# Thirteen instead of eleven attention jobs transpose by DMA, small passes are merged, and a planner's costs and due times are reset

## The chip, the cores and the metric

One NeuronCore of a Trainium2 chip runs the kernel. The time is the device time of one execution in microseconds; the median of several runs counts. The engines are TensorE (PE, with its weight loads PEld), VectorE (DVE), ScalarE (ACT), GpSimd (POOL), SyncE (SP, which issues the DMAs) and 16 DMA engines.

## The reference

Attention with a decay over 4 batches, 8 heads, 576 rows and 64 columns, then two dense layers over the 2304 rows of 512 columns, with 2048 hidden columns each. All is float32.

```python
log_f = np.log(np.clip(f, 0.0001, 1.0))
cum = np.cumsum(log_f, axis=-1)
scores = q @ k.T / sqrt(D) + cum[:, None] - cum[None, :]   # per batch and head
scores = np.where(causal, -1e9, scores)
scores = scores - np.max(scores, axis=-1, keepdims=True)
attn = np.exp(scores); attn = attn / (attn.sum(-1, keepdims=True) + 1e-9)
x = attn @ v                         # heads side by side: (2304, 512)
h = x @ w1_in;  x = (h / (1 + np.exp(-h))) @ w1_out
h = x @ w2_in;  out = (h * np.cos(h)) @ w2_out
```

## The kernel before

**Work.** A job is two heads of one batch; there are 16 pairs. Each pair has two jobs: "a" for rows 0 to 255 and "b" for the last rows, 256 to 575. A job makes scores, decays, a row maximum, an exponential and a sum, a division, a transpose of the weights and the values product. The dense layers go by blocks j of 256 rows (nine of them) and by pairs p of 128 hidden columns (eight), a step (l, j, p) being 24 products into h and those of the second matrix. Numbers that need more than 16 bits are split into two float16 parts and multiplied in three passes (`PASS`); blocks 0 and 1 of the first layer (`J16`) multiply by the second matrix in float32 instead.

**Two kinds of "b" jobs.** `BY_DMA` says which. A job by DMA splits the divided weights into float16 parts (`f_hi`, `f_lo`), transposes them with `dma_start_transpose` on SP's queue (lines 841 and 844, six per job), splits the values, and multiplies in float16 (line 937). The others transpose on TensorE in float32 (lines 810 and 813, 19 products), copy the result out of PSUM, and multiply in float32 (line 948). Before, jobs 0 to 5, 6, 8, 10, 12 and 14 go by DMA.

**Order.** All work is handed to a `Scheduler` as tasks with an engine (or several, `alts`), an assumed duration, dependencies, tokens for buffers (`TOK`) and a key; the smallest key that is ready goes first on each engine. It simulates the run while the kernel is built and so writes out a fixed order for each engine; the hardware only waits on semaphores. The steps of the dense layers have keys from -1000 up and so go before the elementwise work of attention. On TensorE the attention products go first. Where the simulation finds TensorE without work in the first 60 us, it writes a filler product there (`keep_warm`, line 410). `apt` and `better` choose the engine for a task that several can run; `EXTRA` is an extra price of an engine, and before `EARLY` us VectorE takes no such task from another engine. `DSLOW` and `PSLOW` are its assumption for VectorE and GpSimd running beside each other.

**Weights.** They come as 64-bit words, are turned into float32 by a few integer passes (`convert`: lines 479 to 492), squared and summed for a scale, and split. First-layer weights have the key CK0 + CK1 * i for the i-th tile (four tiles per pair p). The second layer's are converted in the background, written to DRAM and loaded again; their i-th load waits for the step W2N0 + int(W2N1 * i) of the first layer.

**Scales.** `scale_tasks` adds two sums of squares, sums them over the partitions with a one-column product (line 429), and makes a power of two and its inverse out of it with three passes on VectorE (lines 434 to 436). `balance` does the like for q and k of a "b" job (lines 593 to 600).

**Decays.** f is clipped, its logarithm taken, and a prefix sum scanned over all 576 columns (lines 447 to 460); the first four "a" jobs read it through a product with a selector (line 768), all others from DRAM.

Of the kernel before, what the change touches and what calls it, by code (L numbers as in the profile page):

```python
# [9 lines left out]
F32 = mybir.dt.float32  # L10
F16 = mybir.dt.float16
BF16 = mybir.dt.bfloat16
# [9 lines left out]
NP = B * H // 2  # L22
# [7 lines left out]
BY_DMA = [n < 6 or n % 2 == 0 for n in range(NP)]  # L30
# [25 lines left out]
KO = {"gs": 1.5, "g2": 1.5, "gl2": 1.5, "cb2": 0.5, "cb3": 0.5, "chi": -2.5, "g": -5.5}  # L56
HAM = 3.4133
# [3 lines left out]
EXTRA = {"DVE": 1.2, "POOL": 0.8}  # L61
# [6 lines left out]
EARLY, LATE = 20, ()  # L68
KDEC, KDP = 12.0, -0.5
# [10 lines left out]
class Scheduler:  # L80
# [35 lines left out]
    def run(self):  # L116
# [56 lines left out]
        while events:  # L173
# [23 lines left out]
            while progress:  # L197
                progress = False
                for e in ENG:
# [41 lines left out]
                    if e == "PE":  # L241
                        w = int(now / HAM)
                        while win < w:
                            warm = work[win] > 0.7 * HAM
                            win += 1
                            if len(work) <= win:
                                work.append(0.0)
                        if not warm:
                            end += best.dur
                        a = now  # L250
                        while a < end - 1e-9:
                            w = int(a / HAM + 1e-9)
# [58 lines left out]
def c_dma(mb):  # L311
    return 0.01 + mb / 0.41
# [3 lines left out]
def decay_attention_silu_cos_kernel(ctx, tc, qa, qb, f, w1i, w1o, w2i, w2o, out):  # L316
# [81 lines left out]
    qe = sb.tile([128, 4], I32, name="qe")  # L398
# [20 lines left out]
    def scale_tasks(i, deps, key, top=15, turns=None):  # L419


        cell = {}

        def f_add():
            nc.vector.scalar_tensor_tensor(sq16[:, i:i + 1], sq[:, 0, i:i + 1], 2.0 ** -60, sq[:, 1, i:i + 1], ALU.max, ALU.add)

        def f_sum():
            cell["n"] = ps.tile([128, 512], F32, tag="s", bufs=TOK["s"], name="nrm")
            nc.tensor.matmul(cell["n"][:, 0:1], ones16, sq16[:, i:i + 1], start=True, stop=True, skip_group_check=True)

        def f_two():
            n = cell["n"][:, 0:1].bitcast(I32)
            a, b = scl[:, i:i + 1].bitcast(I32), inv[:, i:i + 1].bitcast(I32)
            nc.vector.tensor_scalar(b, n, 1, 0x3F800000, ALU.logical_shift_right, ALU.bitwise_and)  # L434
# [12 lines left out]
    def d_ln():  # L447
        nc.vector.tensor_scalar(fc[0:32, 0:S], fc[0:32, 0:S], 1e-4, 1.0, ALU.max, ALU.min)

    def d_scan():  # L450
        nc.vector.tensor_tensor_scan(cum[0:32, 0:S], ones[0:32, 0:S], lf[0:32, 0:S], 0.0, ALU.mult, ALU.add)
        nc.vector.tensor_scalar(cum[0:32, 0:S], cum[0:32, 0:S], -8.0, None, ALU.mult)
# [4 lines left out]
    d1 = add("DVE", 0.95, d_ln, [d0], key=-100)  # L457
    d2 = add("ACT", 0.7, lambda: nc.scalar.activation(lf[0:32, 0:S], fc[0:32, 0:S], AF.Ln), [d1], key=-100)
    add("ACT", 1.4, lambda: nc.scalar.activation(spare, halfpi, AF.Exp), [d2], key=-99)
    d3 = add("DVE", 1.95, d_scan, [d2, dm, dz], key=-100)  # L460
    decay = add("SP", 0.5, lambda: nc.sync.dma_start(decay_d, cum[0:32, 0:S]), [d3], key=KDEC, dma=0.3, name="rows")
    scanned = d3

# [41 lines left out]
    for i in range(2 * NF):  # L505
# [5 lines left out]
        def load(c=c, kind=kind, src=src):  # L511
# [5 lines left out]
                         [decay] if kind == "o" and c >= NF - NT_ else [], kind == "o")  # L517
# [37 lines left out]
    def load_tasks(jb, u):  # L555
# [5 lines left out]
        def tile_of(tag):  # L561
            n, dt = {"qk": (QK, F32), "v": (QB - RB, F32), "dk": (QB, F32)}[tag]
            if beta:
                return sbt(tag, [128, n], dt, name=tag)
            if not half:
                pairs[tag, jb.n // 2] = sbt(tag, [128, n], dt, name=tag)
            return pairs[tag, jb.n // 2]
# [23 lines left out]
        def balance():  # L591
            n, c = jb.n, slice(jb.n, jb.n + 1)
            nc.vector.tensor_scalar(qe[:, 0:nq], jb.qn[:, 0:nq].bitcast(I32), 2, 0x1F800000, ALU.logical_shift_right, ALU.bitwise_and)
            sq_, sk = qsc[:, 0, c].bitcast(I32), qsc[:, 1, c].bitcast(I32)
            nc.vector.scalar_tensor_tensor(sq_, qe[:, 1:2], float(127 << 23), qe[:, 0:1], ALU.add, ALU.subtract)
            nc.vector.tensor_scalar(sk, sq_, -1.0, float(254 << 23), ALU.mult, ALU.add)
# [7 lines left out]
        def norm():  # L604
            jb.qn = ps.tile([128, 512], F32, tag="s", bufs=TOK["s"], name="nrm")
            nc.tensor.matmul(jb.qn[:, 0:nq], ones16, qn.bitcast(BF16).rearrange("p n (c t) -> p n c t", t=2)[:, jb.n, 0:nq, 1], start=True, stop=True, skip_group_check=True)
# [45 lines left out]
        own = beta or not half  # L652
        t0 = add("SP", 0.5, load, key=u, acq=["qs"] if beta else ["qk"] if own else [],
                 deps=[] if own else [jb.mate.loads[2]], dma=c_dma(0.49 if beta else 0.26), name="ldq")
        tv = add("SP", 0.5, load_v, key=u + 0.1, acq=["v"] if own else [], deps=[] if own else [jb.mate.loads[0]],
# [47 lines left out]
        if not beta and jb.n < NS_:  # L703
            if half:
                values.append([tv, jb.mate.loads[0]])
            jb.loads, jb.masked = [tv, tv, t0], {"c01": [masked]}
            return [tl]
        t1 = add("SP", 0.5, decays, [decay] + ([] if own else [jb.mate.loads[1]]), key=u, acq=["dk"] if own else [],
                 dma=1.3 if beta else 1.1, name="ldd")
        jb.loads = [tv, t1, t0]  # L710
# [311 lines left out]
    w1_done, sc1 = {}, []  # L1022
    for p in range(NPR):
        k, key = SW(1, "o", p), C16 + C161 * p
        q = [add(**squares(lambda c=c: wo32[c]["w"], 512, sq[:, c % 2, k:k + 1]), deps=wready[1, "o", c], key=key, name="sqw")
             for c in (2 * p, 2 * p + 1)]
        ts = scale_tasks(k, q, key, 14)
        sc1.append(ts)
# [9 lines left out]
    def f_v1():  # L1038
        i, o = SW(1, "i", 0), SW(1, "o", 0)
        nc.vector.tensor_tensor(v1[:, 0], scl[:, i:i + NPR], scl[:, o:o + NPR], ALU.mult)  # L1040
# [4 lines left out]
    factors1 = add("DVE", 0.9, f_v1, sc1 + [wready[1, "i", 2 * p][0] for p in range(NPR)], key=-500, name="sc")  # L1045
# [4 lines left out]
    for i in range(2 * NF):  # L1050
# [17 lines left out]
        ts = scale_tasks(k, [halves[c - 1][2], halves[c][2]], key, *((15, by) if kind == "i" else (14,)))  # L1068
# [38 lines left out]
    def f_v():  # L1107
        i, o = SW(2, "i", 0), SW(2, "o", 0)
        nc.vector.tensor_tensor(v2[:, 0], scl[:, i:i + NPR], scl[:, o:o + NPR], ALU.mult)
# [4 lines left out]
    factors2 = add("DVE", 0.6, f_v, sc2, key=-500, name="sc")  # L1114
# [47 lines left out]
    def factor_tasks(l, j, ts, key):  # L1162
# [20 lines left out]
        if j < 2:  # L1183
            return [add("DVE", 0.1, f1(p, p + 1), [ts, wts[p]], key=key, name="sc") for p in range(NPR)]
        t = add("DVE", 0.1, f1(0, NPR), [ts] + wts, key=key, name="sc")
# [331 lines left out]
```

## Time and profile before

| | us |
|---|---|
| median of three runs | 912.09 (912.05 to 913.18) |
| the profiled execution | 911.74 |
| its span | 909.9 |

| engine | busy us | share of the span | instructions |
|---|---|---|---|
| TensorE, products | 899.1 | 99% | 7928 |
| TensorE, weight loads | 753.0 | 83% | 7928 |
| VectorE | 760.6 | 84% | 1854 |
| ScalarE | 694.9 | 76% | 1425 |
| GpSimd | 160.7 | 18% | 236 |

A product's end is modelled, so its length says less than the distance of starts. A row of a timeline merges neighbours of one kind: the start of the first, the length until the end of the last, and their count. In brackets stands how long the engine had been idle before, and what ended that. A float32 product counts as two instructions.

### The profile page before, as it was taken

What the parts mean: (1) busy time and instruction counts of PE and PEld (TensorE: products, weight loads), DVE (VectorE), ACT (ScalarE), POOL (GpSimd) and SP (SyncE); (2) the same over time, 40 slices, a digit from 0 to 9 for tenths busy, and PEclk for the clock granted to TensorE, in tenths of its full rate; (3) what the DMA queues carried; (4) which work ended last, traced back from release to release, by engine and by line L of the source; (5) the groups of instructions that cost most, each with busy time, mean ns of one, the idle gap of its engine ahead of it and who ended that gap; (6) DMA issues with size and microseconds to landing.
All of it is one profiled execution on the core that took longest, in us unless ns stands there. A gap on an engine that the chain in (4) does not pass through costs nothing.

```text
span 909.9 us, 20973 instructions
## 1 busy us (share of the span) xinstructions
PE 899.1 (99%) x7928; PEld 753.0 (83%) x7928; DVE 760.6 (84%) x1854; ACT 694.9 (76%) x1425; POOL 160.7 (18%) x236
## 2 busy tenths in 40 slices
PE   9999999999999999999999999999999999999997
PEld 5667777788887888887888888888888888888886
DVE  6899878987876999988899987888888888787775
ACT  7999999876868888788797767766676666666663
POOL 6652321133212324323120100000000000000000
PEclk9999999999999999999999999999999999999999
DMA  8965744967987878886674997000001000000010
GB/s 318 372 223 160 235 151 82 196 142 162 202 191 204 213 215 209 209 191 177 221 233 157 317 355 237 24 24 24 24 24 48 24 24 24 1 25 24 1 24 24
DMA packets 113701, 130.03 MB, mean 143 GB/s; under 512 B 63872, under 2 KB 76160, under 8 KB 113600
## 3 DMA queue, kind: packets, MB, share of 16 engines
q1 hardware_dynamic: 113600, 128.70, 49.2%
q8 instruction: 62, 1.02, 0.5%
q14 instruction: 39, 0.32, 0.1%
HBM read 90.25 MB, written 24.72 MB: 126 GB/s over the span
## 4 chain that ended last, share of the span: by engine, by line
PE 93%; ACT 3%; DVE 2%; DMA 1%; issue 1%; DVEq 0%; ACTq 0%; SPq 0%
PE h L1329 40%; PE y L1441 20%; PE y L1220 18%; PE pv L948 2%; PE spin L410 2%; PE st L762 2%; PE tt L810 2%; PE pv L937 2%; PE st L755 1%; ACT junk L358 1%; PE st L743 1%; PE st L768 1%; DMA rw<-w1i 1%; PE st L742 1%; PE h L1318 0%
## 5 line engine op out<-in xcount | busy, mean ns | idle before, releaser
L1329 PE MATMUL h<-x,wi 128*128 128x256 f16 x3432 | 404.6, 273 | 0.0
L1329 PEld LDWEIGHTS <-wi 128*128 128x128 f16 x3432 | 331.6, 98 | 46.6 <-issue 6.5
L1441 PE MATMUL y<-g,rw 128*128 128x256 f16 (+1 forms) x1600 | 224.1, 292 | 2.7 <-ACT g L333 2.7
L1220 PE MATMUL y<-wo,g 128*128 128x256 f16 x1512 | 176.5, 273 | 0.0
L1220 PEld LDWEIGHTS <-g 128*128 128x128 f16 x1512 | 147.9, 98 | 17.1
L1441 PEld LDWEIGHTS <-rw 128*128 128x128 f16 x1344 | 129.2, 98 | 18.3 <-issue 3.3
L793 ACT ACTIVATE e<-e,su 128x128 f32<-128x128 f32 (+4 forms) x144 | 82.9, 578 | 14.4 <-DVE su L772 14.2
L1383 ACT ACTIVATE t<-h,ru 128x512 f32<-128x512 f32 x72 | 49.2, 684 | 57.8 <-PE h L1329 57.5
L1408 DVE TENSOR_TENSOR g<-t,g 128x896 f16<-128x896 f32 x72 | 78.4, 1089 | 14.9 <-ACT g L1405 13.1
L1405 ACT ACTIVATE g<-t 128x896 f16<-128x896 f32 x72 | 68.0, 944 | 28.8 <-DVE t L1399 28.7
L1393 DVE SCALAR_TENSOR_TENSOR t<-h,rg,t 128x512 f32<-128x512 f32 x72 | 54.0, 749 | 34.7 <-ACT t L1390 34.7
L1389 ACT ACTIVATE t<-t,ru 128x512 f32<-128x512 f32 x72 | 51.7, 717 | 26.7 <-DVE t L1386 26.7
L1354 ACT ACTIVATE t<-h,rg 128x512 f32<-128x512 f32 x72 | 48.9, 680 | 29.3 <-PE h L1329 28.9
L333 ACT ACTIVATE g<-t,rg 128x512 f16<-128x512 f32 (+1 forms) x72 | 51.6, 716 | 22.2 <-PE y L1441 19.4
L772 DVE CUSTOM_DVE_ANT_0 e<-st,dk 128x256 f32<-128x256 f32 (+3 forms) x128 | 59.2, 492 | 8.4 <-PE st L762 3.3
L1386 DVE SCALAR_TENSOR_TENSOR t<-t,ru,h 128x512 f32<-128x512 f32 x72 | 53.5, 743 | 8.9 <-ACT t L1383 8.9
L1357 DVE SCALAR_TENSOR_TENSOR t<-t,h 128x512 f32<-128x512 f32 x72 | 49.2, 683 | 11.9 <-ACT t L1354 11.6
L1441 PEld LDWEIGHTS y<-g,rw 128*128 128x128 f32 x256 | 47.0, 194 | 13.1 <-ACT g L333 3.9
L353 DVE SCALAR_TENSOR_TENSOR g<-t,rg,g 128x512 f16<-128x512 f32 x56 | 43.3, 773 | 13.4 <-ACT g L333 12.8
L1390 ACT ACTIVATE t<-t,halfpi 128x512 f32<-128x512 f32 x72 | 52.0, 722 | 2.3
L834 DVE SCALAR_TENSOR_TENSOR eh<-e,su,eh 128x512 f16<-128x512 f32 (+1 forms) x66 | 41.6, 657 | 1.1 <-ACT eh L333 0.6
L333 ACT ACTIVATE e<-e,su 128x256 f32<-128x256 f32 (+4 forms) x78 | 35.2, 509 | 0.9 <-DVE inv L434 0.5
(158 smaller groups left out, 1260.7 us busy)
## 6 DMA issues: line engine op xcount, KB each, us to landing
rw<-w1i SPq DMA_DIRECT2D x16, 512.0 KB, 5.4
rw<-w1o SPq DMA_DIRECT2D x16, 512.0 KB, 7.3
x<-x_d SPq DMA_DIRECT2D x16, 512.0 KB, 4.2
dk<-decay_d SPq DMA_DIRECT2D x16, 512.0 KB, 4.9
raw<-w2i SPq DMA_DIRECT2D x16, 512.0 KB, 5.0
raw<-w2o SPq DMA_DIRECT2D x16, 512.0 KB, 4.2
qs<-qb SPq DMA_DIRECT2D x16, 480.0 KB, 4.2
w2o_d<-w SPq DMA_DIRECT2D x24, 256.0 KB, 3.3
```

Of the source, the lines that this page charges most:

```text
L333: nc.scalar.activation(dst, src, AF.Copy, scale=scale)
L772: nc.vector.tensor_tensor_reduce(out, s, d, -0.125, first, ALU.add, ALU.min, cell["sm"][:, o:o + 1])
L793: nc.scalar.activation(x, x, AF.Exp, bias=sm[:, i:i + 1], scale=-1.0, accum_out=sm[:, 4 + i:5 + i])
L1220: nc.tensor.matmul(y[bank][:, 256 * half:256 * half + 256], g[:, gi, ga], w[:, wi, 256 * col:256 * col + 256], start=p == 0 and half == 0 ...
L1329: nc.tensor.matmul(h[:, i], w[:, wi, 128 * k:128 * k + 128], x[:, xi, k], start=(i == 0 and q == 0 and k == 0), stop=(i == 1 and q == 2 an ...
L1386: nc.vector.scalar_tensor_tensor(cell["t"], cell["t"], r, cell["h"], ALU.subtract, ALU.subtract)
L1389: nc.scalar.activation(cell["t"], cell["t"], AF.Abs, scale=r)
L1390: nc.scalar.activation(cell["t"], cell["t"], AF.Sin, scale=-2.0 * PI, bias=halfpi)
L1393: nc.vector.scalar_tensor_tensor(cell["t"], cell["h"], r, cell["t"], ALU.mult, ALU.mult)
L1405: nc.scalar.activation(g_t[s][:, 0], cell["w"], AF.Copy)
L1408: nc.vector.tensor_tensor(g_t[s][:, 1], cell["w"], g_t[s][:, 0], ALU.subtract)
L1441: nc.tensor.matmul(y[:, e * TB:(e + 1) * TB], w[:, wi, 128 * ec:128 * ec + 128], g[:, gi, i * TB:(i + 1) * TB], start=(st and e == 0), sto ...
```

## The change

- `BY_DMA`: jobs 7 and 9 go by DMA too, 13 of 16.
- `scale_tasks` can do n scales at once and leave the inverse for later (`late`). The scales of the first layer's second matrix are made four at a time (two products instead of eight), and their inverses and those of the second layer in one call each, in `f_v1` and `f_v`.
- `balance` makes q's and k's scale in one pass: the norm product writes its columns twice.
- Clip, logarithm and prefix sum go in two parts, columns 0 to 255 first; the selector products wait for the first part alone.
- The buffers of "a" jobs are taken by tasks of their own with an early key.
- "b" jobs have a key lower by `LEAD` = 1, and their three units are `USTEP` = 1.5 apart instead of 2. `GAP4`, a pause of keys before the second batch of "a" jobs, goes from 8 to 5.
- The planner's numbers: extra price of GpSimd 0.8 to 2.0, `EARLY` 20 to 60, keys of weights, key offsets by name (`KO`), a window for its clock model shifted by `HAM0`.

```diff
-BY_DMA = [n < 6 or n % 2 == 0 for n in range(NP)]
+BY_DMA = [n < 11 or n % 2 == 0 for n in range(NP)]
-LOOK = 12
+LOOK = 13
-QD = 3
+QD = 4.0
-CK2 = 12
+CK2 = 18
-GAP4, GAP8 = 8, 12
-CK0, CK1 = 10, 1.6
-C2K0, C2K1 = 150, 0.5
-W2N0, W2N1 = 30, 1.0
-J16, C16, C161 = 2, 70, 2.0
+GAP4, GAP8 = 5, 12
+CK0, CK1 = 12, 1.8
+C2K0, C2K1 = 210, 0.2
+W2N0, W2N1 = 37, 0.8
+J16, C16, C161 = 2, 65.0, 3.5
-KO = {"gs": 1.5, "g2": 1.5, "gl2": 1.5, "cb2": 0.5, "cb3": 0.5, "chi": -2.5, "g": -5.5}
-HAM = 3.4133
+KO = {"gs": 1.5, "g2": 1.5, "gl2": 1.5, "cb2": 1.5, "cb3": 1.0, "chi": 1.0, "g": -6.5, "max": -3.0, "ldq": -0.5, "exp": 0.5, "xc": 4, "nm": -3.0, "rec": -4, "clo": -2.0, "ws": 4, "qhi": 4, "sqw": -0.5, "cb1": 4, "ldd": -0.5, "hide": 1.5, "tc": 0.5, "vhi": 4, "cexp": 1.5, "qlo": 0.5}
+HAM, HAM0 = 3.4133, 1.3
-EXTRA = {"DVE": 1.2, "POOL": 0.8}
+EXTRA = {"DVE": 1.2, "POOL": 2.0}
-EARLY, LATE = 20, ()
-KDEC, KDP = 12.0, -0.5
+EARLY, LATE = 60, ()
+KDEC, KDP = 6, 0.5
+LEAD, USTEP, GAPB = 1, 1.5, 0
...
-    def scale_tasks(i, deps, key, top=15, turns=None):
+    def inverse(i, n, top):
+        b = inv[:, i:i + n].bitcast(I32)
+        nc.vector.tensor_scalar(b, b, 1.0, float((65 - top) << 23), ALU.mult, ALU.add)
+
+    def scale_tasks(i, deps, key, top=15, turns=None, n=1, late=False):
...
-            nc.vector.tensor_scalar(b, b, 1.0, float((65 - top) << 23), ALU.mult, ALU.add)
+            if not late:
+                inverse(i, n, top)
...
+    def d_scan(a, b):
+        def f():
+            nc.vector.tensor_tensor_scan(tot[0:32, a:b], ones[0:32, a:b], lf[0:32, a:b],
+                                         tot[0:32, a - 1:a] if a else 0.0, ALU.mult, ALU.add)
+            nc.vector.tensor_scalar(cum[0:32, a:b], tot[0:32, a:b], -8.0, None, ALU.mult)
+        return f
...
+    scanned = add("DVE", 0.9, d_scan(0, 256), [d2, dm, dz], key=-100)
...
-            sp = load_tasks(jb, pos)
+            sp = load_tasks(jb, pos - (LEAD if kind == "b" else 0))
...
-                    un += unit_tasks(jb, u, pos + 2 * i, sp, [])
+                    un += unit_tasks(jb, u, pos + USTEP * i, sp, [])
...
+            ts = scale_tasks(k, q, C16 + C161 * (p + NQ - 1), 14, n=NQ, late=True)
```

## Rows read from the trace of the kernel before

**Rows 1.** Stretches: busy PE, PEld, DVE, ACT, POOL (instructions), clock, DMA share, GB/s.

```profile
7.00:30.00 23.00, 23.00 (x148) 14.27 (x146) 17.13 (x61) 19.82 (x62) 16.44 (x20) 1.00 1.00 368
...
66.50:75.00 8.50, 5.01 (x18) 3.87 (x18) 8.19 (x27) 8.50 (x24) 2.85 (x4) 0.80 0.62 189
...
75.00:130.00 55.00, 55.00 (x417) 43.06 (x415) 45.19 (x156) 54.87 (x165) 15.19 (x22) 1.00 0.58 171
130.00:446.00 316.00, 316.00 (x2866) 255.03 (x2864) 271.09 (x742) 257.23 (x576) 89.70 (x140) 1.00 0.77 186
446.00:555.00 109.00, 108.93 (x1009) 97.20 (x1008) 95.50 (x227) 82.26 (x157) 12.21 (x16) 1.00 0.78 265
555.00:902.60 347.60, 347.26 (x3186) 310.90 (x3184) 283.95 (x544) 231.42 (x334) 0.00 (x0) 1.00 0.09 29
```

**Rows 2.** TensorE's timeline around 188 and 278 to 293: start, length, what.

```profile
188.56 1.97 PE L1441 MATMUL y<-g,rw 128*128 128x256 f32 x8
...
278.50 1.87 PE L937 MATMUL pv<-pt 128*64 128x320 f16 x30
280.30 1.09 PE L810 MATMUL tt<-ident,e 128*128 128x128 f32 x8
281.23 0.27 PE L742 MATMUL st<-qk 128*128 128x256 f16 x1
...
290.47 2.42 PE L948 MATMUL pv<-pt,v 128*64 128x320 f32 x20
292.82 0.82 PE L762 MATMUL st<-qk 64*128 64x512 f16 x6
```

**Rows 3.** Line 410 (fillers) by stretch: PE, PEld, clock, DMA share, GB/s.

```profile
0.00:30.00 30.00, 16.88 (x60) 6.18 (x60) 1.00 0.92 326
30.00:46.00 16.00, 7.42 (x29) 2.68 (x29) 1.00 1.00 385
```

**Rows 4.** TensorE's timeline around the hole at 66 to 75.

```profile
58.12 2.86 PE L1441 MATMUL y<-g,rw 128*128 128x256 f32 x12
60.81 0.82 PE L810 MATMUL tt<-ident,e 128*128 128x128 f32 x6
...
67.33 0.16 PE L429 MATMUL nrm<-sq,ones 128*128 128x1 bf16 x1 [1.01 <-DVE inv L434]
70.15 4.54 PE L1441 MATMUL y<-g,rw 128*128 128x256 f32 x12 [2.65 <-ACT g L333]
```

**Rows 5.** DMA issues of the whole run: count, median us to landing.

```profile
pt<-eh SPq DMA_TRANSPOSE x66, 3.4
```

**Rows 6.** VectorE by line, 225 to 450: count, busy us, mean ns.

```profile
L834 DVE SCALAR_TENSOR_TENSOR eh<-e,su,eh 128x512 f16<-128x512 f32 (+2 forms) x42 | 26.3, 651 | 0.8 <-POOL eh L335 0.5 <-ACT eh L333 0.3
...
L700 DVE SCALAR_TENSOR_TENSOR pt<-v,scl,pt 128x512 f16<-128x512 f32 (+1 forms) x12 | 6.3, 568 | 0.3 <-ACT pt L333 0.3
...
L596 DVE TENSOR_SCALAR qsc<-qsc 128x1 int32<-128x1 int32 x10 | 1.5, 154 | 0.3
```

**Rows 7.** VectorE's timeline at the start.

```profile
2.73 0.94 DVE L448 TENSOR_SCALAR fc<-fc 32x576 f32<-32x576 f32 x1 [1.24 <-DMA fc<-f]
4.49 1.48 DVE L451 TENSOR_TENSOR_SCAN cum<-ones,lf 32x576 f32<-32x576 f32 x1 [0.82 <-ACT lf L458]
6.00 0.45 DVE L452 TENSOR_SCALAR cum<-cum 32x576 f32<-32x576 f32 x1
```

**Rows 8.** TensorE's timeline, 6.8 to 9.

```profile
6.87 2.12 PE L410 MATMUL spin<-ones 128*128 128x512 bf16 x9
8.82 1.47 PE L768 MATMUL st<-cum,sel 128*128 128x128 f32 x8
```

**Rows 9.** Chain that ended last, before 80 us: start, us, what.

```profile
52.51 5.45 DMA rw<-w1i
```

**Rows 10.** Line 335, 60 to 200 us, sum of the stretches.

```profile
sum 140.00, DVE 2.99 POOL 15.47; mean DVE 0.43 POOL 2.21
```

**Rows 11.** Line 1058, loads of the second layer: issue, first and last start.

```profile
L1058 SPq DMA_DIRECT2D raw<-w2i x16: 332/422/802, 275.0 to 510.2; - x16
```

More of the change, by code (lines that the diff above doesn't have):

```diff
@@ L241, in run @@
                     if e == "PE":
-                        w = int(now / HAM)
+                        w = int((now + HAM0) / HAM)
                         while win < w:
@@ L427, in f_sum @@
         def f_sum():
             cell["n"] = ps.tile([128, 512], F32, tag="s", bufs=TOK["s"], name="nrm")
[L429 removed]
+            nc.tensor.matmul(cell["n"][:, 0:n], ones16, sq16[:, i:i + n], start=True, stop=True, skip_group_check=True)
         def f_two():
[L432 to L434 removed]
+            m = cell["n"][:, 0:n].bitcast(I32)
@@ L440, in scale_tasks @@
         t = add("PE", 0.04, f_sum, [t], key=key - 10000.0, acq=["s"], name="sc")
-        return add("DVE", 0.46, f_two, [t], key=key, rel=["s"], name="sc")
+        return add("DVE", 0.31 if late else 0.46, f_two, [t], key=key, rel=["s"], name="sc")
     fc, lf, ones, cum = [sb.tile([128, 1024], F32, tag=f"wo{NF - NT_ + i}", bufs=1, name=n)
                          for i, n in enumerate(("fc", "lf", "ones", "cum"))]
-    def d_ln():
-        nc.vector.tensor_scalar(fc[0:32, 0:S], fc[0:32, 0:S], 1e-4, 1.0, ALU.max, ALU.min)
@@ L516, in decay_attention_silu_cos_kernel @@
                          dict(rel=["raw"]) if kind == "i" else dict(rel=["lo"]), [],
-                         [decay] if kind == "o" and c >= NF - NT_ else [], kind == "o")
+                         [decay] if kind == "o" and (c >= NF - NT_ or c == NF - NT_ - 2) else [], kind == "o")
         if kind == "o" and c >= NF - NT_ - 1:
@@ L564, in tile_of @@
                 return sbt(tag, [128, n], dt, name=tag)
-            if not half:
+            if (tag, jb.n // 2) not in pairs:
                 pairs[tag, jb.n // 2] = sbt(tag, [128, n], dt, name=tag)
@@ L605, in norm @@
             jb.qn = ps.tile([128, 512], F32, tag="s", bufs=TOK["s"], name="nrm")
-            nc.tensor.matmul(jb.qn[:, 0:nq], ones16, qn.bitcast(BF16).rearrange("p n (c t) -> p n c t", t=2)[:, jb.n, 0:nq, 1], start=True, stop=True, skip_group_check=True)
+            n = qn.bitcast(BF16).rearrange("p n (c t) -> p n c t", t=2)[:, jb.n, 0:nq, 1]
+            nc.tensor.matmul(jb.qn[:, 0:2 * nq], ones16, n.unsqueeze(1).to_broadcast([128, 2, nq]), start=True, stop=True,
+                             skip_group_check=True)
         def rows(a, heads, count, copies):
@@ L650, in decayt @@
                 nc.sync.dma_start(jb.dt[64 * a:64 * a + 64], rows(a, 1, S, 64))
[L652 to L655, printed above, removed]
+        at = {}
+        if not beta:
+            at = jb.mate.at if half else {tag: add("SP", 0.0, lambda: None, key=u - 300, acq=[tag], name="at")
+                                          for tag in (["qk", "v", "dk"] if jb.n >= NS_ else ["qk", "v"])}
+            jb.at = at
+        t0 = add("SP", 0.5, load, key=u, acq=["qs"] if beta else [], deps=[] if beta else [at["qk"]],
+                 dma=c_dma(0.49 if beta else 0.26), name="ldq")
+        tv = add("SP", 0.5, load_v, key=u + 0.1, acq=["v"] if beta else [], deps=[] if beta else [at["v"]],
                  dma=c_dma(0.33 if beta else 0.13), name="ldq")
@@ L704, in load_tasks @@
             if half:
-                values.append([tv, jb.mate.loads[0]])
-            jb.loads, jb.masked = [tv, tv, t0], {"c01": [masked]}
+                values.append([tv, jb.mate.tv])
+            jb.tv, jb.masked = tv, {"c01": [masked]}
             return [tl]
-        t1 = add("SP", 0.5, decays, [decay] + ([] if own else [jb.mate.loads[1]]), key=u, acq=["dk"] if own else [],
+        t1 = add("SP", 0.5, decays, [decay] + ([] if beta else [at["dk"]]), key=u, acq=["dk"] if beta else [],
                  dma=1.3 if beta else 1.1, name="ldd")
-        jb.loads = [tv, t1, t0]
         r = [tl, tv, t1]
@@ L997, in decay_attention_silu_cos_kernel @@
             mate = jb
-            sp = load_tasks(jb, pos)
+            if kind == "b" and jb.n == 0:
+                pos += GAPB
+            sp = load_tasks(jb, pos - (LEAD if kind == "b" else 0))
             if kind == "a":
@@ L1022, in decay_attention_silu_cos_kernel @@
     w1_done, sc1 = {}, []
+    NQ = 4
     for p in range(NPR):
         k, key = SW(1, "o", p), C16 + C161 * p
[L1025 to L1028, printed above, removed]
+        if p % NQ == 0:
+            q = [add(**squares(lambda c=c: wo32[c]["w"], 512, sq[:, c % 2, k + c // 2 - p:k + c // 2 - p + 1]),
+                     deps=wready[1, "o", c], key=C16 + C161 * (c // 2), name="sqw") for c in range(2 * p, 2 * p + 2 * NQ)]
+            ts = scale_tasks(k, q, C16 + C161 * (p + NQ - 1), 14, n=NQ, late=True)
+            sc1.append(ts)
         for c in (2 * p, 2 * p + 1):
@@ L1044, in f_v1 @@
         nc.vector.tensor_scalar(rg3, v1[:, 1], vm[:, 2:3], 2.0 ** -16, ALU.mult, ALU.mult)
-    factors1 = add("DVE", 0.9, f_v1, sc1 + [wready[1, "i", 2 * p][0] for p in range(NPR)], key=-500, name="sc")
+    factors1 = add("DVE", 1.05, f_v1, sc1 + [wready[1, "i", 2 * p][0] for p in range(NPR)], key=-500, name="sc")
     w2_done = {}
@@ L1067, in decay_attention_silu_cos_kernel @@
         by = sq2[:, p:p + 1] if kind == "i" else scl[:, k:k + 1]
-        ts = scale_tasks(k, [halves[c - 1][2], halves[c][2]], key, *((15, by) if kind == "i" else (14,)))
+        ts = scale_tasks(k, [halves[c - 1][2], halves[c][2]], key, *((15, by) if kind == "i" else (14,)), late=True)
         sc2.append(ts)
@@ L1113, in f_v @@
         nc.vector.tensor_scalar(rg2, v2[:, 1], vm[:, 0:1], 2.0 ** -16 / INV2PI, ALU.mult, ALU.mult)
-    factors2 = add("DVE", 0.6, f_v, sc2, key=-500, name="sc")
+    factors2 = add("DVE", 1.2, f_v, sc2, key=-500, name="sc")
     steps = {}
@@ L1183, in factor_tasks @@
         if j < 2:
-            return [add("DVE", 0.1, f1(p, p + 1), [ts, wts[p]], key=key, name="sc") for p in range(NPR)]
-        t = add("DVE", 0.1, f1(0, NPR), [ts] + wts, key=key, name="sc")
+            return [add("DVE", 0.2, f1(p, p + 1), [ts, wts[p]], key=key, name="sc") for p in range(NPR)]
+        t = add("DVE", 0.2, f1(0, NPR), [ts] + wts, key=key, name="sc")
         return [t] * NPR
```

41 lines of the change are left out of this document (24 added, 17 removed).

## The prediction

> **What bounds the kernel now.** I read the busy times by stretch first, then TensorE's timeline. In the table by stretch the reader is to see one engine without holes: TensorE is busy 55.00 of 55.00 us from 75 to 130, 316.00 of 316.00 from 130 to 446, 108.93 of 109.00 from 446 to 555 and 347.26 of 347.60 from there to its last product, at a granted clock of 1.00 [rows 1]. So from 75 us on nothing but TensorE's own work sets the end, and an edit counts there only if it takes products away, or if it makes something so late that a hole opens.
>
> The share of busy time alone would not prove that, since ends of products are modelled. By the Trainium skill's Perfetto Trace Analysis, section Identifying the Most-Contended Engine, a busy matmul row is a poor measure of headroom. By that rule removed products might give nothing back; the starts in the timeline decide against it here: 30 products of a values pass begin at 278.50 and the next group begins at 280.30, at once behind them, with no idle time noted [rows 2].
>
> Before 75 us it is otherwise. TensorE is kept busy there with filler products (line 410) that compute nothing: 60 of them up to 30 us and 29 more up to 46 us, 16.88 and 7.42 us of busy time. In the same time the DMA engines are busy 0.92 and 1.00 of the time [rows 3], and ScalarE 19.82 of 23 us from 7 to 30 us [rows 1]: the start is held by loads, by ScalarE and by the chain of the first jobs. From 66.5 to 75 us the clock falls to 0.80 [rows 1]. The timeline shows how: TensorE is idle for 1.01 us before the second of two norm products, then 2.65 us for ScalarE's g, and 12 products of the second matrix last 4.54 us where 12 such, 58.12 to 60.81, had needed 2.69 [rows 4]. That hole costs 1.01 + 2.65 + (4.54 - 2.69) = 5.5 us. The clock stood at its 2.4 GHz level before it, and the 12 products behind it ran in good part at the 1.2 GHz level.
>
> **The change part by part.**
>
> Two more jobs (7 and 9) over the crossbar. Such a job drops its 19 transposes on TensorE, and its float32 values pass becomes the float16 one. In the job shown, 8 transposes go from 280.30 to 281.23, 0.116 us each; 19 are 2.2 us. Its float32 values pass goes from 290.47 to 292.82, 2.35 us; the float16 pass takes 280.30 - 278.50 = 1.80 us [rows 2]. The score products are the same in both kinds. Per job 2.2 + 2.35 - 1.80 = 2.75 us less, for two jobs 5.5 us, all of it on the path by rows 1. I take -5.5; the lower bound is 0, if TensorE must wait in their place.
>
> What these jobs add lies beside TensorE. Six crossbar transfers each, 3.4 us from issue to landing, on SP's queue [rows 5]; behind them on that queue wait loads of later jobs, rows and weights. Twelve more transfers stand beside 66 that left TensorE without a hole. VectorE gets six more passes of line 834 at 0.651 us and two of line 700 at 0.568 us [rows 6], 5.0 us per job, 10 us in all, and it has 316 - 271.09 = 45 us free in that stretch [rows 1]. The merged tiny passes give about as much back: 8 norms become two (6 x 3 passes less), the inverses of 24 scales are made in three calls (21 less), and each of 16 jobs drops one pass; 55 passes at 0.154 us, that of the one dropped in each job [rows 6], are 8.5 us. Cost 0; if the cover were gone, the 10 us would be late at the rows of block 7, not on TensorE at once.
>
> Here a rule speaks against the change. By the Trainium skill's VectorE: DVE Perf Modes, section The three transpose paths, a 128x128 bf16 transpose takes 390 ns on TensorE and 1309 ns over the crossbar; if both lay on the path, 19 of them would make a job 19 x 0.92 = 17.5 us longer (an estimate from that page), 35 us for two. The trace has the eleven jobs' transfers off the path, and the sum goes by that.
>
> Six norm products of the second matrix fall away: one is 0.16 us long [rows 4], but such products run into the next one. Between 0 and 1.0 us; I take 0, as they have one column where a step's product has 256.
>
> The prefix sums in two halves. Today the first decay products wait for the whole of clip, logarithm, scan and scaling: from 2.73 to 6.45 us on VectorE [rows 7]. A first half of 256 of 576 columns costs 256/576 of 0.94 + 1.48 + 0.45 us, 1.3 us, plus ScalarE's half and the handovers, about 2 us: ready near 4.8 us instead of 6.45. The decay products start at 8.82 us today, behind nine fillers that the written order put there (6.87 to 8.82) [rows 8]. They can move up to the end of the score products, so at most 1.95 us are won, at least 0 if the fillers stay. ScalarE is nearly full from then on [rows 1], so a start earlier by so much moves the stage. I take -1.9, near the upper end, because the fillers are put in only where the kernel's own planner sees nothing ready.
>
> The written order of the first 130 us. Jobs of the second and third batch move forward by 3 places, first-layer weights back (the pair p from 10 + 6.4p to 12 + 7.2p), and other priorities change. The hole of 5.5 us hangs on one such order: in the chain of waits it begins at a weight load of 5.45 us that starts at 52.51 [rows 9]. A new order can close it (-5.5), or leave one like it (0), or make a second (+5.5). I take half of the hole, -2.7, as nothing in the trace ranks the orders; the ends stay for the range.
>
> GpSimd gets fewer shared passes. From 60 to 200 us it ran 15.47 us of line 335's passes [rows 10]. If all went to ScalarE, which has 0.13 us free from 75 to 130 [rows 1], the last first-half jobs would be some 10 us later (15.47 us of GpSimd, scaled by about two thirds as ScalarE is the quicker). Nobody on TensorE waits for them then: the float32 steps of the first two blocks still run until 190.4 us (188.56 + 1.8) [rows 2]. Cost 0; 10 us if that cover were gone.
>
> Later jobs of the last rows start 4 places earlier and their units are 1.5 places apart instead of 2; the second layer's weights start 7 steps later (today's first load is at 275.0 us [rows 11]) and end at the same step. Both move work among engines with room. VectorE has 109 - 95.5 = 13.5 us free from 446 to 555 [rows 1]. Cost 0, upper end about 5 us at the seam of the layers.
>
> Sum: the profiled execution takes 911.74 us (span 909.9), 0.35 below the median of the runs. 911.74 - 5.5 - 1.9 - 2.7 = 901.6, and with the 0.35 of the median 902.0.
>
> **The rivals.**
>
> A, only the products go. The start is redrawn at the same price, with a hole like today's: 912.09 - 5.5 = 906.6, and up to 909 if the two jobs open small waits. For it: the start is bound by DMA (1.00 busy from 30 to 46 us [rows 3]), which no edit relieves. Against: fillers and a hole are there to be won.
>
> B, the start becomes much tighter: hole gone, decays earlier, and a third of the 24.3 us of fillers replaced by real products (8 us, of which 1.9 are counted): 902.0 - 2.7 - 6.1 = 893.2. For it: 30 us of fillers and hole are on the path. Against: real products need rows and weights, and these need loads.
>
> C, slower: weights too late. The place is 46 to 130 us, where TensorE lives on the steps of blocks 0 and 1, each of which needs its pair of weights. The last pair goes back by 7.6 places, nearly four jobs, and ScalarE passes the jobs first; it is full there (54.87 of 55.00 us [rows 1]). A step missing leaves holes of the kind seen, 5.5 us each with the lower clock behind it. Three of them instead of one are 11 us more: 912.09 - 5.5 - 1.9 + 11 = 915.7. It decides once TensorE runs dry for 7.4 us (5.5 + 1.9) more than today in that stretch. For it: the one hole today goes back to such a weight [rows 9]. Against: each job moved forward brings its own products.
>
> D, the crossbar's latency lies on the path, so that the values products wait for the transfers: 3.4 us for each of six transfers in two jobs, 41 us against 5.5 saved if none were covered, 912.09 - 5.5 + 41 = 947.6. Against: TensorE busy 316.00 of 316.00 us with eleven such jobs. The rule on transpose paths above would point this way.
>
> E, the change does nothing that counts: the two jobs' waits eat the 5.5 us, the start stays. 911 to 913.
>
> **How the numbers follow.** The forecast (896 to 905) 0.48; A (905 to 909.5) 0.22; B (below 896) 0.16; C 0.08; D 0.01; E 0.05. The likeliest one's own range is 896 to 905. To hold 8 of 10 I take 893 to 909.5: about half of B lies below it, and C, D and E above. About 0.2% (1.8 us) is what a measurement of this kernel tells from no change. Faster: forecast, A and B, 0.86. Same: most of E, 0.04. Slower: C, D and the rest of E, 0.10.
>
> **What would show it.** Right: 13 jobs' transfers (78 instead of 66), 150 transposes of line 810 instead of 186 (18 a job there, one in line 813), 3 float32 values passes of the last rows instead of 5, TensorE without a hole from some point before 80 us to its last product, first decay products near 7 us, fewer than 89 fillers. Wrong: a hole behind 130 us before a values pass or at the seam of the layers, more fillers than 89, or a second fall of the clock between 46 and 130 us.

## The result, and the profile after

The changed kernel takes 904.88 us (904.57 to 905.51) against 912.31 us of the kernel before on the same chip: a ratio of 0.9918, 95% interval 0.9901 to 0.9935, or 7.4 us less. The forecast was 902.0 us. The profiled execution takes 904.93 us with a span of 903.1.

The busy times by stretch of the changed kernel, the columns and stretches as in [rows 1] (the last two end earlier by what was won):

```profile
7.00:30.00 23.00, 23.00 (x147) 13.72 (x146) 18.02 (x64) 21.16 (x67) 16.35 (x23) 1.00 1.03 397
...
66.50:75.00 8.50, 7.03 (x42) 4.54 (x41) 8.29 (x20) 8.47 (x25) 1.90 (x2) 1.00 0.41 123
...
75.00:130.00 55.00, 54.93 (x407) 42.44 (x405) 50.73 (x161) 54.80 (x160) 12.09 (x17) 1.00 0.63 191
130.00:446.00 316.00, 315.72 (x2897) 256.54 (x2896) 276.23 (x748) 264.50 (x587) 37.51 (x83) 1.00 0.80 191
446.00:548.00 102.00, 101.86 (x943) 91.01 (x942) 89.46 (x213) 79.69 (x154) 5.13 (x6) 1.00 0.80 276
548.00:896.00 348.00, 347.53 (x3188) 311.29 (x3188) 287.35 (x552) 232.81 (x337) 0.00 (x0) 1.00 0.09 31
```

TensorE is still full from 75 us on; the waits noted there are 0.22 us before the last values pass (431.40) and 0.47 us at the seam of the layers (551.17). The clock between 66.5 and 75 us is 1.00 instead of 0.80. VectorE and ScalarE are a little busier from 130 to 446 us, GpSimd falls there from 89.70 to 37.51 us.

The fillers (now line 411) by stretch, as in [rows 3]:

```profile
0.00:30.00 30.00, 15.08 (x54) 5.28 (x54) 1.00 0.94 345
30.00:46.00 16.00, 4.12 (x16) 1.48 (x16) 1.00 1.01 397
```

70 instead of 89. Part of the reason stands at the start of TensorE's timeline (compare [rows 8]):

```profile
5.00 1.65 PE L773 MATMUL st<-qk 64*128 64x128 f32 x8
6.59 1.58 PE L786 MATMUL st<-cum,sel 128*128 128x128 f32 x8
```

The first decay products begin at 6.59 us instead of 8.82. But the hole of [rows 4] is not gone for nothing. TensorE's timeline after it, in the changed kernel:

```profile
51.10 1.24 PE L966 MATMUL pv<-pt,v 128*64 128x256 f32 x8 [0.81 <-ACT pt L334]
...
54.55 0.89 PE L828 MATMUL tt<-ident,e 128*128 128x128 f32 x4 [0.35 <-POOL e L336]
56.08 0.44 PE L828 MATMUL tt<-ident,e 128*128 128x128 f32 x2 [0.64 <-POOL e L336]
...
60.04 1.13 PE L1466 MATMUL y<-g,rw 128*128 128x256 f32 x4 [0.96 <-ACT g L334]
...
67.71 1.53 PE L828 MATMUL tt<-ident,e 128*128 128x128 f32 x6 [0.34 <-ACT e L334]
...
72.46 0.16 PE L434 MATMUL nrm<-sq,ones 128*128 128x1 bf16 x1 [0.82 <-DMA rw<-w1i]
```

Waits of 0.3 to 1 us stand in brackets, and a group can hold one inside: six transposes took 1.53 us from 67.71, where [rows 2] has eight in 0.93.

If each group is given the time to the start of the next one, less the idle time noted, over the whole of both timelines, this is where TensorE's time changed:

| TensorE's time, us | before | after | change |
|---|---|---|---|
| transposes (191, 153) | 21.5 | 19.9 | -1.6 |
| values passes, float32 | 24.6 | 20.7 | -3.9 |
| values passes, float16 | 19.8 | 23.4 | +3.6 |
| fillers | 22.1 | 17.8 | -4.3 |
| second matrix, float32 | 60.2 | 58.5 | -1.7 |
| first half's scores and selector products | 19.5 | 20.5 | +1.0 |
| idle time noted behind the start | 4.0 | 4.8 | +0.8 |
| all others | | | -0.6 |

The rounded rows add up to -6.7 us; the span changed by -6.8. At the 0.1126 us that a transpose (one instruction) took before, 38 fewer are -4.3; only -1.6 came out, so 2.7 us of waiting lie inside the groups of transposes. The two jobs' products are these 38 transposes (-4.3), 40 float32 instructions of the values passes (2 x 2.35 us by [rows 2], -4.7) and the float16 passes in their place (+3.6): -5.4 us. (The table's -3.9 holds 0.8 us by which the first half's float32 passes, line 966 with 256 columns, were lengthened; the three of the last rows that are left are as long as before.)

The start can be read by itself from the same two timelines, as an estimate good to about half a microsecond: give each product that is not a filler the median distance to the next start among its kind in both kernels, and add these up in order. TensorE reaches 45 us of such real work at 71.4 us instead of 74.3, and 150 us of it at 178.7 instead of 180.4. So the lead is 2.9 us at first and 1.7 us in the end; the rest of the gain comes later, where the two jobs' products are missing. This measure is used again below.

The transfers, as in [rows 5]:

```profile
pt<-eh SPq DMA_TRANSPOSE x78, 3.5
```

### The profile page after: what moved, and what is told of

It is laid out like the page before. It is cut to its first block, busy times and chain, and to the rows that moved or that the text cites. A ratio compares the mean times of both kernels' runs of the same rounds, so it can differ in the third digit from the quotient of the medians.

```text
span 903.1 us, 20845 instructions
## 1 busy us (share of the span) xinstructions
PE 890.9 (99%) x7885; PEld 746.0 (83%) x7885; DVE 766.6 (85%) x1867; ACT 702.1 (78%) x1441; POOL 105.2 (12%) x176
## 4 chain that ended last, share of the span: by engine, by line
PE 84%; ACT 7%; DVE 4%; DMA 4%; issue 1%; SPq 0%; DVEq 0%; ACTq 0%
PE h L1354 38%; PE y L1466 19%; PE y L1245 18%; PE pv L955 2%; PE st L780 2%; DMA rw<-w1i 2%; ACT e L811 1%; PE pv L966 1%; DMA w2i_d<-w 1%; ACT junk L359 1%; PE tt L828 1%; ACT e L334 1%; PE st L761 1%; PE st L760 1%; DVE w L506 1%
## 5 line engine op out<-in xcount | busy, mean ns | idle before, releaser
L334 ACT ACTIVATE g<-t,rg 128x512 f16<-128x512 f32 (+1 forms) x72 | 51.5, 715 | 19.4 <-PE y L1466 17.8
L852 DVE SCALAR_TENSOR_TENSOR eh<-e,su,eh 128x512 f16<-128x512 f32 (+1 forms) x78 | 47.5, 634 | 4.4 <-ACT eh L334 4.2
L334 ACT ACTIVATE eh<-e,su 128x512 f16<-128x512 f32 (+2 forms) x65 | 37.5, 608 | 1.8 <-DMA w2i_d<-w 1.0
```

The lines of the kernel that those rows point to most:

```text
L334: nc.scalar.activation(dst, src, AF.Copy, scale=scale)
```

## The experiments

The kernel before took 911.9 to 912.0 us beside these experiments and 912.31 beside the result, so differences from the changed kernel's 904.88 are sure to about 0.4 us.

Two theories stood against each other at first. P: TensorE's own products set the end, so that each part has a price and the prices add up. O: the order is written out by a planner, any edit deals it anew, and holes decide.

**One part alone, put on the kernel before.** Jobs 7 and 9 over the crossbar (transposed by DMA):

```diff
-BY_DMA = [n < 6 or n % 2 == 0 for n in range(NP)]
+BY_DMA = [n < 11 or n % 2 == 0 for n in range(NP)]
```

> The kernel before with jobs 7 and 9 over the crossbar and nothing else. Theory P (what counts is TensorE's own products): 2 x 2.7 us of products go and the rest of the order stays about as it is, 912.3 - 5.4 = 906.9, with 89 fillers as before and the hole at 66 to 75 us still there. Rival O (the written order is dealt anew by any edit, and holes before 130 us move the time by several us either way): more than 2 us away from 906.9.

933.43 us, ratio 1.0236 (1.0221 to 1.0252): over 26 us more than P says. The start is as before, with 89 fillers and the same hole. The time is lost elsewhere, as TensorE's timeline of this kernel shows:

```profile
457.62 2.42 PE L948 MATMUL pv<-pt,v 128*64 128x320 f32 x20
...
475.83 0.19 PE L429 MATMUL nrm<-sq,ones 128*128 128x1 bf16 x1 [9.38 <-DVE sq L425]
...
481.43 6.96 PE L1329 MATMUL h<-x,wi 128*128 128x256 f16 x48 [1.01 <-ACT x L333]
```

The last values pass of the last rows begins at 457.62 us, and TensorE then waits 9.38 us. The wait ends with the squares of a second-layer weight (ScalarE, 474.85), which the written order puts ahead of block 7's first step; the step itself waits until 481.43 for ScalarE's pass over the block's rows. ScalarE's timeline shows that these rows were no earlier than the weight:

```profile
474.85 0.63 ACT L358 ACTIVATE junk<-w 128x512 bf16<-128x512 f32 x1 [1.60 <-DVE w L492]
476.19 0.63 ACT L358 ACTIVATE junk<-x 128x512 bf16<-128x512 f32 x1 [0.62 <-DMA x<-x_d]
...
480.67 1.93 ACT L333 ACTIVATE x<-x,scl 128x512 f16<-128x512 f32 x3
```

With the smaller waits beside it 18 us of idle time stand between 450 and 500 us, and the clock is 0.81 from 446 to 500. Who is late stands in the queue of loads. The last values pass of the last rows, the load of block 7's rows and TensorE's first products on them, in the kernel before, in the changed one, and the load in this one:

```profile
443.75 2.42 PE L948 MATMUL pv<-pt,v 128*64 128x320 f32 x20
...
451.06 1.19 SPq L1191 DMA_DIRECT2D x<-x_d  x2
...
464.51 1.47 PE L1329 MATMUL h<-x,wi 128*128 128x256 f16 x12
```

```profile
431.40 2.42 PE L966 MATMUL pv<-pt,v 128*64 128x320 f32 x20 [0.22 <-ACT pt L334]
...
441.94 0.88 SPq L1216 DMA_DIRECT2D x<-x_d  x2
...
454.83 1.47 PE L1354 MATMUL h<-x,wi 128*128 128x256 f16 x12
```

```profile
468.38 1.61 SPq L1191 DMA_DIRECT2D x<-x_d  x2
```

Before, the load is issued at 451.06 and TensorE begins block 7 at 464.51 without a wait. With two more crossbar jobs alone it is issued at 468.38. The changed kernel has it at 441.94 and begins block 7 at 454.83. So a second deadline stands behind TensorE's: the last rows' jobs, fed by VectorE and ScalarE, must end before TensorE reaches block 7 (its last 64 rows come from the last batch's "b" jobs). The theory from here on is S: the extra passes are paid for by the room before this deadline, and before the next, the seam of the layers, where the second layer's weights must be ready.

**The same part taken out of the changed kernel.**

```diff
-BY_DMA = [n < 11 or n % 2 == 0 for n in range(NP)]
+BY_DMA = [n < 6 or n % 2 == 0 for n in range(NP)]
```

> The changed kernel with jobs 7 and 9 back on TensorE. Theory P: 904.9 + 5.4 = 910.3, with 70 fillers and the start as in the changed kernel. Rival O: more than 2 us away from it.

910.22 us, ratio 0.9979 (0.9970 to 0.9988); 70 fillers, a start like that of the changed kernel. 5.3 us are what P says, to 0.2. Inside the changed kernel the two jobs are worth their products. The same run prices all the rest of the change: it has the products of the kernel before but for a few norms, and that kernel took 911.93 us beside it, so the rest wins 1.7 us.

**The numbers alone on the kernel before.**

```diff
-LOOK = 12
+LOOK = 13
-EXTRA = {"DVE": 1.2, "POOL": 0.8}
+EXTRA = {"DVE": 1.2, "POOL": 2.0}
...
```

(and in the same way QD, CK2, GAP4, CK0, C2K0, W2N0, J16's line, KO, EARLY and KDEC; not LEAD, USTEP and HAM0)

> The kernel before with the changed kernel's planner numbers (weights' keys, pauses, priorities, EXTRA, EARLY, depth of loads), but with its old jobs, scan, scales and clock window. Theory P: the numbers only re-deal the first 75 us; the start of the changed kernel is worth 1.5 us net, and the decays come late as before, so 911 to 912.5. Rival N (the numbers carry the gain in fillers, 4.3 us): 907 to 908.5.

915.73 us, ratio 1.0043 (1.0029 to 1.0056): slower than either says. 88 fillers are left, and the hole behind 66 us grew:

```profile
71.51 2.08 PE L1441 MATMUL y<-g,rw 128*128 128x256 f32 x4 [3.03 <-ACT g L333]
```

But the last values pass begins at 431.39 us instead of 443.75, and the load of block 7 at 439.85. The numbers alone lose 3.8 us against the 911.93 beside them; they move the last rows forward by 12 us. I read that as the room that two more crossbar jobs need.

**The prefix sums in halves, alone on the kernel before.** The new functions `d_ln`, `d_log` and `d_scan` with their tasks, nothing else:

```diff
-    d3 = add("DVE", 1.95, d_scan, [d2, dm, dz], key=-100)
+    scanned = add("DVE", 0.9, d_scan(0, 256), [d2, dm, dz], key=-100)
...
+    d3 = add("DVE", 1.15, d_scan(256, S), [d2, scanned], key=-99)
```

> The kernel before with the prefix sums in two halves and nothing else. Theory P as predicted: the first decay products start near 7 us instead of 8.8 and fillers fall by some 1.9 us: 912.3 - 1.9 = 910.4. Rival: the start is held by loads and ScalarE, fillers come back later, 912.3 within 0.5.

937.97 us, ratio 1.0287 (1.0273 to 1.0301). The part itself does what was forecast: the first decay products come at 7.10 us, and the fillers fall to 77. From TensorE's timeline and from its lines:

```profile
7.10 1.58 PE L776 MATMUL st<-cum,sel 128*128 128x128 f32 x8
...
477.92 0.18 PE L429 MATMUL nrm<-sq,ones 128*128 128x1 bf16 x1 [8.40 <-DVE sq L425]
```

```profile
L410 PE MATMUL spin<-ones 128*128 128x512 bf16 x77 | 21.3, 418 | 1.1 <-DVE ones L372 1.1
```

The gain does not even last through the start: TensorE reaches 22 us of real work 1.9 us earlier than before (at 42.97 us), as forecast, but 60 us of it 0.9 us later (at 90.35). So the start is held elsewhere, as the rival says. The large loss is at block 7: the last values pass begins at 463.71 us, 20 us later than before, and TensorE waits 8.40 us in one place. The jobs that it needs there come later by the new order; why is not shown.

**Jobs 7 and 9 with later weights of the second layer.** On the first experiment:

```diff
-C2K0, C2K1 = 150, 0.5
-W2N0, W2N1 = 30, 1.0
+C2K0, C2K1 = 210, 0.2
+W2N0, W2N1 = 37, 0.8
```

> The kernel before with jobs 7 and 9 over the crossbar (which alone took 933.4 us and left a hole of 18 us behind 466 us), and with the second layer's weights loaded and converted later (first load 7 steps later, keys from 210). Theory S (that hole is the last rows' jobs ending too late for block 7, because the second layer's weight passes share VectorE and ScalarE with them): the last values pass ends before 446 us, the hole goes, 912.1 - 5.4 = 906.7 within 1.5. Rival W (the extra passes of the two jobs alone make them late, whatever the weights do): 925 to 933, hole still there.

924.35 us, ratio 1.0137 (1.0122 to 1.0152): neither number, 0.65 us below W's range. The last values pass begins at 448.19 instead of 457.62, and the hole there shrinks to 9.7 us. A second one opens at the seam:

```profile
466.41 0.19 PE L429 MATMUL nrm<-sq,ones 128*128 128x1 bf16 x1 [6.85 <-DVE sq L425]
...
566.03 2.56 PE L1329 MATMUL h<-x,wi 128*128 128x256 f16 x16 [4.30 <-DVE t L1393]
```

So the second layer's weights do take part in the lateness, as S says, but half of the hole stays without them, as W says, and later weights push part of the lack to the seam.

**All 16 jobs over the crossbar, on the changed kernel.**

```diff
-BY_DMA = [n < 11 or n % 2 == 0 for n in range(NP)]
+BY_DMA = [True for n in range(NP)]
```

> The changed kernel with all 16 jobs over the crossbar. Theory P alone: three more jobs save 3 x 2.7 us, 904.9 - 8.1 = 896.8. Theory S: in the kernel with only jobs 7 and 9 added, two jobs made the last values pass 12 us later (457.6 instead of 445), so three make it some 18 us later, 431.4 + 18 = 449.4; the load of block 7's rows, at 441.9 in the changed kernel, comes near 460, where TensorE needs it by some 453: a hole of 5 to 10 us with a fall of the clock, 902 to 910.

926.09 us, ratio 1.0160 (1.0147 to 1.0174), with the mechanism that S names but not its size: the last rows are less late than S said (444.81 us, not 449.4), and the holes cost more:

```profile
444.81 1.87 PE L955 MATMUL pv<-pt 128*64 128x320 f16 x30
...
454.47 0.16 PE L434 MATMUL nrm<-sq,ones 128*128 128x1 bf16 x1 [5.03 <-DVE sq L430]
...
462.42 0.16 PE L434 MATMUL nrm<-sq,ones 128*128 128x1 bf16 x1 [7.79 <-DVE sq L430]
```

The last values pass moved by 13.4 us and the load of block 7 to 455.25; 16.9 us of idle time stand between 450 and 500 us and 7.9 us behind 550. In the table by stretch the DMA engines are at 0.98 from 350 to 400 us, and the clock falls to 0.84:

```profile
350.00:400.00 50.00, 50.00 (x485) 41.09 (x482) 46.11 (x122) 41.16 (x94) 10.47 (x18) 1.00 0.98 220
...
446.00:500.00 54.00, 36.96 (x323) 30.98 (x320) 46.03 (x110) 42.51 (x87) 1.97 (x3) 0.84 0.68 231
```

**One more job only.** `n < 13` instead of `n < 11`:

> The changed kernel with 14 jobs over the crossbar (job 11 too). Theory P: one more job saves 2.7 us, 902.2. Theory S: one job makes the last rows some 6 us later; the rows of block 7 were loaded at 441.9 us in the changed kernel and are needed by some 453, so no hole opens there and 902.2 comes out within 1; if VectorE's five more us are late at the seam of the layers instead, 905 to 910.

912.51 us, ratio 1.0003 (0.9994 to 1.0012). Block 7 is in time (its load is at 440.76), and the lack comes at the seam:

```profile
550.60 0.16 PE L434 MATMUL nrm<-sq,ones 128*128 128x1 bf16 x1 [4.26 <-DVE sq L430]
...
553.74 6.53 PE L1354 MATMUL h<-x,wi 128*128 128x256 f16 x32 [2.97 <-DVE t L1418]
```

The first wait is for the squares of a second-layer block's rows, the second for the elementwise work of the first step. VectorE does the scale of the last pair of weights only at 546.3 us and then tiny factor passes, which need the scales of all pairs, until 549.1; the elementwise work of a step and the sum of the squares (550.39) come behind them. I read the scale of the last pair as the deadline at the seam. 7.2 us of idle time and the clock behind it (0.94 from 548 to 640 us) cost more than the 2.7 us of products. The changed kernel waits 0.47 us there itself: its margin at the seam is gone already.

**GpSimd's old extra price in the changed kernel.**

```diff
-EXTRA = {"DVE": 1.2, "POOL": 2.0}
+EXTRA = {"DVE": 1.2, "POOL": 0.8}
```

> The changed kernel with GpSimd's old extra price (0.8), so that it takes many shared passes after 60 us again. Theory S: more passes of GpSimd slow VectorE beside it; if the last rows still end before some 450 us the time stays, 904.9 within 1. Rival G (the fewer passes of GpSimd are part of the gain): 908 or more, with a hole behind 440 us.

911.41 us, ratio 0.9995 (0.9986 to 1.0004): rival G. The first deadline is met (last values pass at 429.84), the seam is not:

```profile
549.91 0.16 PE L434 MATMUL nrm<-sq,ones 128*128 128x1 bf16 x1 [2.14 <-DVE sq L430]
...
552.85 7.07 PE L1354 MATMUL h<-x,wi 128*128 128x256 f16 x48 [2.78 <-DVE t L1418]
```

GpSimd's groups of line 499 (a pass over the second layer's weights) from 300 to 548 us, in the kernel with the old price and in the changed one, count first, then busy time and mean:

```profile
L499 POOL TENSOR_SCALAR raw<-raw 128x512 int32<-128x512 uint16 x21 | 17.3, 825 | 82.3 <-DMA raw<-w2i 25.8 <-DVE t L1382 21.7 <-DMA raw<-w2o 13.9
```

```profile
L499 POOL TENSOR_SCALAR raw<-raw 128x512 int32<-128x512 uint16 x8 | 6.8, 852 | 40.8 <-DVE t L1382 29.7 <-ACT junk L359 7.8 <-DMA raw<-w2o 1.6
```

With the old price GpSimd takes 21 of them instead of 8, and some of VectorE's passes take longer beside it (line 1120 from 446 to 548 us: 479 ns instead of 416). What of the 6.5 us is longer passes and what is order was not separated.

**The prefix sums whole again.** The functions of before in the changed kernel:

> The changed kernel with the prefix sums whole again, as before. Predicted part: the two halves are worth 1.9 us, 904.9 + 1.9 = 906.8, with the first decay products near 8.8 us and some 5 fillers more. Rival O (order dealt anew): anything more than 2 us away from 906.8.

911.02 us, ratio 0.9996 (0.9986 to 1.0005), 6.1 us more than the changed kernel where 1.9 were forecast. Fillers rise to 85:

```profile
L411 PE MATMUL spin<-ones 128*128 128x512 bf16 x85 | 22.1, 406 | 1.1 <-DVE ones L373 1.1
```

15 fillers more are 2.9 us of busy time, and the first decay products begin at 7.52 us, not near 8.8 as forecast. But the fillers are not the price: TensorE reaches 22 us of real work 2.5 us later than in the changed kernel, but 45 us of it only 0.5 us later. It falls back again between 88 and 111 us and reaches 150 us of work 3.1 us later (181.8); and 3.3 us of idle time stand behind 150 us where the changed kernel has 0.7. This looks like rival O more than like the part's own price.

**The tiny passes as before.** `NQ = 1`, no `late`, and the old `balance`:

> The changed kernel with the tiny passes as before (a norm for each pair of the second matrix, an inverse after each scale, q's and k's scale in two passes): some 8.5 us more of VectorE's work. Theory P: off the path, 904.9 within 1. Theory S (the second layer's weights end just in time at the seam of the layers, so that VectorE's time there counts): a hole behind 540 us or at block 7, 907 or more.

912.95 us, ratio 1.0012 (1.0003 to 1.0021): S. The order is dealt anew here too (the first decay products begin at 5.74 us), so the 8.1 us are not the passes' time alone. The last values pass begins at 440.27 and block 7's load at 450.77; TensorE waits for that block's squares:

```profile
461.92 0.18 PE L434 MATMUL nrm<-sq,ones 128*128 128x1 bf16 x1 [2.57 <-DVE sq L430]
...
467.72 0.16 PE L434 MATMUL nrm<-sq,ones 128*128 128x1 bf16 x1 [0.94 <-DVE sq L430]
```

**No fillers.**

```diff
-FILL1 = 60
+FILL1 = 0
```

> The changed kernel without filler products. If fillers stand only where TensorE has nothing to do, the 19 us of them become idle time; the granted clock then falls in the first 46 us, and the products there take up to twice as long. Theory P: the start is held by loads and ScalarE, so slower products hide there: 904.9 to 907. Rival H (the lower clock lengthens the first jobs' chain): 908 or more.

914.85 us, ratio 1.0035 (1.0022 to 1.0049): the number is rival H's, 10 us more than the changed kernel, but the start is as P says. The clock is 0.94 in the first 30 us, and TensorE reaches 22 us of real work 3.2 us later than in the changed kernel; but it reaches 60 us of it 0.4 us earlier, and 300 us of it at 326.5 against 326.2. The whole price stands at block 7, whose rows' jobs come later (last values pass 439.72 instead of 431.40):

```profile
0.00:30.00 30.00, 19.64 (x113) 13.30 (x114) 21.95 (x73) 24.20 (x66) 17.44 (x29) 0.94 0.93 344
...
446.00:548.00 102.00, 94.22 (x842) 82.00 (x841) 93.40 (x219) 78.42 (x153) 5.17 (x6) 0.97 0.79 276
```

```profile
461.22 0.16 PE L434 MATMUL nrm<-sq,ones 128*128 128x1 bf16 x1 [2.80 <-DVE sq L430]
...
463.31 0.16 PE L434 MATMUL nrm<-sq,ones 128*128 128x1 bf16 x1 [1.93 <-DVE sq L430]
```

The planner counts with the clock too, so the order differs as well. TensorE's progress up to 326 us thus owes nothing measurable to the fillers; whether the last rows' jobs are late because of the lower clock or because of the other order is not shown.

**The first-layer weights' keys as before.**

```diff
-GAP4, GAP8 = 5, 12
-CK0, CK1 = 12, 1.8
+GAP4, GAP8 = 8, 12
+CK0, CK1 = 10, 1.6
```

> The changed kernel with the first-layer weights' keys and the pause before the second batch as before (CK0, CK1, GAP4). Rival C of the prediction said that later weights cost time between 46 and 130 us: if so, 904.9 minus 1 to 3 here. If the forward jobs earn what the later weights cost: 904.9 to 908, with more fillers and the waits of 46 to 75 us gathered in one hole.

907.82 us, ratio 0.9958 (0.9946 to 0.9971), 2.9 us more than the changed kernel. The small waits gather in one hole again, with the clock at 0.80 from 66.5 to 75 us, and TensorE reaches 45 us of real work 2.1 us later (73.45). That is made good by 300 us of work (326.1 against 326.2); the 2.9 us come at the seam, with waits of 1.68 us at 549.11 and 1.26 at 553.15. The hole:

```profile
69.44 2.94 PE L1466 MATMUL y<-g,rw 128*128 128x256 f32 x8 [2.87 <-ACT g L334]
```

No version tried is faster than the changed kernel.

## Why the prediction was right, and where its steps were not

- **The two jobs (-5.5).** Right: 5.3 by the experiment that takes them out of the changed kernel, 5.4 by TensorE's groups. Their transfers stay off the path; rival D is out. The counts came as named: 78 transfers, 150 transposes of what was line 810, three float32 values passes of the last rows.
- **The decays (-1.9).** Right in place: they begin 2.2 us earlier, and the fillers fell by 4.3 us in all. But the step from there to the time failed: "a start earlier by so much moves the stage". Put on the old kernel alone, the 1.9 us are there after 22 us of real work and gone after 60. The whole run lost 26 us with it, and 6.1 us without it in the changed kernel; I read both as mostly the order, dealt anew.
- **The hole (-2.7).** This is the term that failed most. Start and hole together were to win 1.9 + 2.7 = 4.6 us; all of the change but the two jobs won 1.7 (911.93 - 910.22). By TensorE's table the jobs gave -5.4 and the fillers -4.3 instead of -1.9; all that has to do with waits gave +3.0 instead of -2.7. The lower clock did go (float32 steps -1.7), but the waits came back in pieces: +2.7 inside transposes (most of it between 46 and 85 us), +0.8 inside the first half's values passes, +1.0 in the first scores (before 30 us), +0.8 noted as idle (all others -0.6). -5.4 - 4.3 + 3.0 = -6.7, against -6.8 by the spans. "Half of the hole" was a mean of two ends where the trace ranked neither.
- **Rival A, 906.6 us,** lies 1.7 us from the result, the forecast 2.9, and the result is 0.1 us inside the 905 where A's range begins. So the time does not tell the two apart, and that it fell on the forecast's side is luck. A says that the start is redrawn at the same price; the start's 1.7 us lie between A's 0 and the forecast's 4.6, nearer to A.
- **Rival C, weights too late.** Out: with the old keys the kernel is slower, and it reaches 45 us of real work 2.1 us later, not earlier.
- **The parts costed at nothing.** Here the reasons failed, though the sum did not. I counted VectorE's free time in a stretch (45 us from 130 to 446) and called added or removed passes free. The experiments show two deadlines inside, block 7's rows at 455 to 465 us and the seam near 550: putting 8.5 us of tiny passes back cost 8.1, GpSimd's old price 6.5, one more crossbar job 7.6 instead of -2.7, with the order dealt anew in each. That the parts at nothing did cost nothing is luck too, as the changed kernel has no margin left at the seam. I had written that lateness would show "at the rows of block 7, not on TensorE at once"; it does show there, and for the two jobs alone at 21.5 us net. A rival on the slower side should have been this one, its price a hole and the clock behind it.
- The parts, each taken out of the changed kernel, cost 5.3, 6.1, 6.5, 8.1 and 2.9 us, 28.9 together, against 7.4 that the whole change wins. They don't add up. I read that as holes hiding one another at the same two deadlines, but each part was taken out with the planner's numbers left as they were, so its price holds the order dealt anew as well. Theories S and O are not rivals to the end: S says where the time is lost, O why the jobs come late, and only for the two jobs does the price match the products alone. Why the order of the kernel before makes the last rows 14 to 20 us later for a single part is not settled, and an edit that only deals the order anew was not tried.

## What to carry to other kernels

Where one engine is full, an edit that saves its time is worth it only if everything that it will need comes as much earlier. Look for deadlines, not for free time: for each stage the last input, when it is ready and when it is needed; the smaller of these margins is the cover, and one edit in an order written out by a planner moved the last rows by 14 to 20 us here (their last values pass at 457.62 and 463.71 instead of 443.75). A part tested alone on the old kernel can lose 20 us and still be worth its full price in the new one (the two jobs: 21.5 us lost, 5.3 won), so test it by taking it out as well; and where the time moves, find by the work done at several points whether it moved at the part or at a later deadline.

## What was not expected of the hardware

A hole costs more than its idle time because the clock falls behind it: in the first experiment 20 us of idle time between 350 and 500 us came with a granted clock of 0.81 from 446 to 500. The same idle time went with different clocks: between 46 and 75 us the changed kernel idles 4.1 us in pieces of at most 0.96 us, and the clock stays at 1.00; with the old weights' keys it idles 4.1 us too, 2.87 of it in one piece, and the clock is 0.80 from 66.5 to 75 us. And with all 16 jobs over the crossbar the median crossbar transfer took 3.5 us to landing, as with 13, while the DMA engines were busy 0.98 of the time from 350 to 400 us.
